# Output stores of a decay-attention and two-MLP kernel: one store of both batches, or one store per batch

## The chip, the core and the metric

The kernel runs on one core of a Trainium2 chip. The time is the device time of one execution in microseconds; the figure of the kernel before is the median of three runs. The profile is one profiled execution on the same kind of core, and all positions in it are microseconds from the start of its span.

## The reference

Three parts follow one another. Attention with an exponential decay runs over blocks of 64 positions, with a state carried from block to block, for 2 batches, 8 heads, 768 positions and 64 values per head. Its output is laid out as 1536 rows (batch, then position) of 512 values. Two MLPs follow.

```python
for b in range(nb):                       # blocks of 64 positions
    intra = einsum('bhij,bhjd->bhid', einsum('bhic,bhjc->bhij', qb, kb) * Dmask, vb)
    inter = einsum('bhid,bhde->bhie', qb * lam_pow, kv_state)
    out[:, :, sl] = intra + inter
    kv_state = lam_block * kv_state + einsum('bhsd,bhse->bhde', kb * rev_pow, vb)
x = out.transpose(0, 2, 1, 3).reshape(1536, 512)
h = x @ w_in;   x = (h * clip(h + 3, 0, 6) / 6) @ w_out       # first MLP, 512 -> 2048 -> 512
h = x @ w_in2;  out = maximum(0.01 * h, h) @ w_out2           # second MLP
```

## The kernel before

**Tiling.** The 1536 tokens are cut into three token tiles of 512 (`NTT` = 3), and each token tile holds 256 positions of both batches. Inside a token tile the tokens stand in four pieces (`SPT` = 4) of 128: 64 positions of batch 0 and the same 64 positions of batch 1. The hidden width of 2048 is cut into 16 slices of 128, which are grouped into blocks (`BLOCKS`). For each layer the work goes over blocks, in a block over token tiles, and in a token tile over the block's slices. One step is one slice on one token tile: a first product (`gemm1`, line 427, 12 matmuls), the gate on ScalarE and VectorE (lines 435 to 462), and a second product (`gemm2`, line 485, 12 matmuls) into four PSUM banks. Each fp32 operand is kept in two parts, so a product takes three matmuls.

**Sums.** When a block is done for a token tile, `collect` (line 496) adds each PSUM bank to the running sum `SUM[t][:, e, :]` in SBUF, one VectorE instruction of 128x512 for each of the four pieces e. In the second layer the 128 partitions of such a piece are tokens: partitions 0 to 63 are batch 0 (`own[0]`) and 64 to 127 are batch 1 (`own[1]`), and the 512 columns are the output values. In the last block of the second layer the sum is final, and `store(t, e)` (lines 510 to 513) sends it to the output. A store takes 128 rows of 2 KB from SBUF to two places of 64 contiguous rows each in the output, 768 rows apart. There are 12 stores, four for each token tile.

**Order.** The class `Order` is a list scheduler that runs while the program is built: it simulates engine times and due times and so fixes the order in which each engine gets its instructions. Every DMA of this kernel, load or store, is issued from SyncE's queue (SP). A store is added with `after=[c]`, c being the `collect` of its piece; nothing comes after a store, and no buffer is given back by it. The program ends (line 584, the end of the tile context) when SP has seen all DMAs land and the engines have met.

## Time and profile before

| | |
|---|---|
| median of 3 runs | 625.24 us (624.1 to 626.78) |
| profiled execution, span from first to last instruction | 622.5 us |
| profiled execution, time outside the span | the page gives none |
| TensorE matmul busy | 581.2 us (93%) |
| VectorE busy | 414.1 us (67%) |
| ScalarE busy | 272.4 us (44%) |
| GpSimd busy | 50.3 us (8%) |
| read from HBM, written to HBM | 45.88 MB, 3.15 MB |

The page's rows of tenths cut the span into 40 slices of 15.6 us; a digit is the busy share of an engine, and the DMA row is the mean busy share of the core's 16 DMA engines. The three runs and the profiled execution are different executions; the difference of 2.7 us between the median and the span holds what lies before the first and after the last instruction, and the spread from run to run.

### The profile page before, as it was taken

What the parts mean: (1) busy time and instruction counts of PE and PEld (TensorE: products, weight loads), DVE (VectorE), ACT (ScalarE), POOL (GpSimd) and SP (SyncE); (2) the same over time, 40 slices, a digit from 0 to 9 for tenths busy, and PEclk for the clock granted to TensorE, in tenths of its full rate; (3) what the DMA queues carried; (4) which work ended last, traced back from release to release, by engine and by line L of the source; (5) the groups of instructions that cost most, each with busy time, mean ns of one, the idle gap of its engine ahead of it and who ended that gap; (6) DMA issues with size and microseconds to landing.
All of it is one profiled execution on the core that took longest, in us unless ns stands there. A gap on an engine that the chain in (4) does not pass through costs nothing.

```text
span 622.5 us, 8825 instructions
## 1 busy us (share of the span) xinstructions
PE 581.2 (93%) x3562; PEld 483.2 (78%) x3562; DVE 414.1 (67%) x654; ACT 272.4 (44%) x460; POOL 50.3 (8%) x43
## 2 busy tenths in 40 slices
PE   7778799999999999999999999999999999999950
PEld 6568777888888888888888888888888888888840
DVE  8999999879479926985289962886469423442420
ACT  2356556775256424653266643672255222222200
POOL 3853540000000000000000000000000000000000
PEclk8978999999999999999999999999999999999985
DMA  8745652333103300330013120221011000001111
GB/s 285 241 156 184 203 173 75 112 120 105 65 35 115 122 0 23 113 120 16 2 35 135 68 101 1 95 108 68 2 58 44 1 1 1 0 12 51 49 47 46
DMA packets 16193, 49.60 MB, mean 80 GB/s; under 512 B 1944, under 2 KB 1944, under 8 KB 16152
## 3 DMA queue, kind: packets, MB, share of 16 engines
q1 hardware_dynamic: 16152, 49.03, 22.8%
q8 instruction: 28, 0.46, 0.3%
q14 instruction: 13, 0.11, 0.1%
HBM read 45.88 MB, written 3.15 MB: 79 GB/s over the span
## 4 chain that ended last, share of the span: by engine, by line
PE 86%; DVE 7%; DMA 3%; issue 0%; SPq 0%; DVEq 0%
PE h L427 42%; PE acc L485 35%; PE a L485 6%; DMA raw<-w 2%; DVE t L381 1%; DVE t L383 1%; PE a L273 1%; PE a L292 1%; DVE r L264 1%; PE a L258 1%; DVE t L373 1%; DVE xl L304 1%; DVE t L370 1%; DMA vs<-vv 1%; DVE sum L496 0%
## 5 line engine op out<-in xcount | busy, mean ns | idle before, releaser
L427 PE MATMUL h<-xh,wh 128*128 128x512 f32 (+1 forms) x396 | 153.3, 387 | 1.2 <-DVE xl L304 1.2
L427 PE MATMUL h<-xl,wh 128*128 128x512 f32 (+1 forms) x396 | 152.7, 386 | 0.2 <-DVE xl L304 0.2
L427 PE MATMUL h<-xh,wl 128*128 128x512 f32 (+1 forms) x396 | 152.6, 385 | 0.0
L427 PEld LDWEIGHTS h<-xh,wh 128*128 128x128 f32 x396 | 75.5, 191 | 16.1 <-ACT t L364 1.4
L452 ACT ACTIVATE gh<-u 128x512 fp32r<-128x512 f32 (+1 forms) x99 | 61.2, 620 | 61.0 <-DVE u L446 32.6
L427 PEld LDWEIGHTS h<-xh,wl 128*128 128x128 f32 x396 | 75.5, 191 | 14.7
L427 PEld LDWEIGHTS h<-xl,wh 128*128 128x128 f32 x396 | 75.4, 191 | 14.7 <-DVE xl L304 0.3
L446 DVE TENSOR_TENSOR u<-u,h 128x512 f32<-128x512 f32 x48 | 32.8, 684 | 65.1 <-ACT u L437 65.1
L437 ACT ACTIVATE u<-h 128x512 f32<-128x512 f32 x48 | 28.7, 598 | 105.7 <-PE h L427 105.5
L485 PE MATMUL acc<-gh,wh 128*128 128x512 f32 (+1 forms) x178 | 68.1, 383 | 2.8 <-DVE xl L304 2.8
L485 PE MATMUL acc<-gl,wh 128*128 128x512 f32 (+1 forms) x178 | 67.1, 377 | 0.0
L485 PE MATMUL acc<-gh,wl 128*128 128x512 f32 (+1 forms) x178 | 66.9, 376 | 0.0
L435 ACT ACTIVATE u<-h,three 128x512 f32<-128x512 f32 (+1 forms) x51 | 33.8, 663 | 73.1 <-PE h L427 72.9
L485 PE MATMUL acc<-wh,gh 128*128 128x512 f32 x160 | 62.2, 389 | 0.0
L485 PE MATMUL acc<-wl,gh 128*128 128x512 f32 x160 | 62.2, 389 | 0.0
L485 PE MATMUL acc<-wh,gl 128*128 128x512 f32 x160 | 62.2, 389 | 0.0
L391 ACT CAST wh<-t 128x512 fp32r<-128x512 f32 x64 | 39.5, 621 | 51.8 <-DVE t L383 45.5
L444 DVE SCALAR_TENSOR_TENSOR u<-u,h 128x512 f32<-128x512 f32 (+1 forms) x51 | 33.2, 652 | 26.9 <-ACT u L435 26.7
L383 DVE CUSTOM_DVE_ANT_0 t<-t,c 128x1024 uint16<-128x1024 uint16 x64 | 48.6, 760 | 2.2
L496 DVE TENSOR_TENSOR sum<-acc,sum 128x512 f32<-128x512 f32 x60 | 39.3, 684 | 16.1 <-PE acc L485 16.1
L381 DVE SCALAR_TENSOR_TENSOR t<-raw,t 128x512 uint32<-128x512 uint32 x64 | 47.6, 744 | 1.4
L360 ACT ACTIVATE c<-raw 128x512 uint32<-128x512 uint32 x64 | 42.7, 667 | 8.6 <-DMA raw<-w 8.6
(75 smaller groups left out, 759.1 us busy)
## 6 DMA issues: line engine op xcount, KB each, us to landing
raw<-w SPq DMA_DIRECT2D x64, 512.0 KB
q<-qkk SPq DMA_DIRECT2D x12, 512.0 KB
vs<-vv SPq DMA_DIRECT2D x24, 128.0 KB
out<-sum SPq DMA_DIRECT2D x12, 256.0 KB
k<-qkk SPq DMA_DIRECT2D x11, 256.0 KB
lam_sb<-lam SPq DMA_DIRECT2D x1, 4.0 KB
```

What stands on the lines that cost most here:

```text
L360: nc.scalar.activation(out=CV[h][1], in_=RAW[h][:, :, 0], func=AF.Copy, scale=2.0 ** -29)
L381: nc.vector.scalar_tensor_tensor(out=t, in0=RAW[h][:, :, 1], scalar=0xC0000000, in1=t, op0=ALU.bitwise_and, op1=ALU.bitwise_or)
L383: nc.vector.tensor_tensor(out=t, in0=t, in1=c, op=ALU.add)
L391: nc.scalar.copy(out=cut(*h, 0), in_=CV[h][0].bitcast(F32))
L427: nc.tensor.matmul(ps, a[:, 0, ws], x[:, k, :], start=(n == 0), stop=(n == 3 * KC - 1))
L435: nc.scalar.activation(out=U[s], in_=PH[s], func=AF.Relu, bias=three, scale=1.0)
L437: nc.scalar.activation(out=U[s], in_=PH[s], func=AF.Copy, scale=0.01)
L444: nc.vector.scalar_tensor_tensor(out=g, in0=U[s], scalar=6.0, in1=PH[s], op0=ALU.min, op1=ALU.mult)
L446: nc.vector.tensor_tensor(out=g, in0=U[s], in1=PH[s], op=ALU.max)
L452: nc.scalar.activation(out=G[s][0], in_=U[s], func=AF.Copy, scale=1.0 / 6.0 if steps[s][0] == 0 else 1.0)
L485: nc.tensor.matmul(ACC[e], a, x, start=(first and n == 0), stop=(last and n == 2))
L496: nc.vector.tensor_tensor(out=acc, in0=ps, in1=acc, op=ALU.add)
```

## The change

A store of 128 rows becomes two stores of 64 rows, one for each batch, each from one half of the partitions to 64 contiguous rows of the output. For the token tiles 0 and 1 both are issued from SP. For the last token tile the one of batch 0 is issued from SP and that of batch 1 from ScalarE's queue (ACT). The comments of the file are taken out too, with the line numbers kept up to line 510.

```diff
     def store(t, e):
         c0 = (t * SPT + e) * C
-        rows = out.rearrange("(b s) m -> b s m", b=B)[:, c0:c0 + C, :]
-        return lambda _: nc.sync.dma_start(out=rows, in_=SUM[t][:, e, :])
+
+        def fn(_):
+
+            for b in range(B):
+                queue = nc.scalar if b and t == NTT - 1 else nc.sync
+                queue.dma_start(out=out[b * S + c0:b * S + c0 + C, :], in_=SUM[t][own[b], e, :])
+        return fn
```

On SP's queue the end of the program reads as follows; `raw` are the weights, `sum_100` to `sum_102` the sums of the token tiles 0 to 2, and the shape is that of the transfer. Lines with - are of before, with + of the changed kernel.

```order
 L232 DMA vs<-vv 64x512 x2
 L353 DMA raw<-w 128x1024 x52
-L513 DMA out<-sum_100 2x64x512 x4
-L513 DMA out<-sum_101 2x64x512 x4
-L513 DMA out<-sum_102 2x64x512 x4
-L584 UNCONDITIONAL_BRANCH
+L517 DMA out<-sum_100 64x512 x8
+L517 DMA out<-sum_101 64x512 x8
+L517 DMA out<-sum_102 64x512 x4
+L589 UNCONDITIONAL_BRANCH
```

Twelve transfers with three dimensions become twenty with two, behind the same last weight load. On ScalarE, at the end of its program, where `u` and `gh` belong to the gate of the last steps:

```order
 L437 ACTIVATE u<-h 128x512
 L452 ACTIVATE gh<-u 128x512
-L584 UNCONDITIONAL_BRANCH
+L517 DMA out<-sum_102 64x512 x4
+L589 UNCONDITIONAL_BRANCH
```

Four transfers stand behind ScalarE's last arithmetic instruction, and nothing but the end of the program behind them. On TensorE, VectorE and GpSimd the order of the instructions is the same in both kernels.

## Rows read from the trace of the kernel before

**Rows 1.** The page: the span, TensorE's line, and of the 40 slices TensorE's busy tenths, the DMA engines' tenths and what they moved.
```profile
span 622.5 us, 8825 instructions
...
PE   7778799999999999999999999999999999999950
...
DMA  8745652333103300330013120221011000001111
GB/s 285 241 156 184 203 173 75 112 120 105 65 35 115 122 0 23 113 120 16 2 35 135 68 101 1 95 108 68 2 58 44 1 1 1 0 12 51 49 47 46
DMA packets 16193, 49.60 MB, mean 80 GB/s; under 512 B 1944, under 2 KB 1944, under 8 KB 16152
```

**Rows 2.** The chain of work that ended last, its last pieces in order of time: start, length, what.
```profile
588.55 2.04 PE acc L485 x9
590.59 2.72 PE h L427 x12
593.31 4.09 PE acc L485 x18
597.40 0.02 issue
597.43 2.73 DVE sum L496 x4
```

**Rows 3.** The waits of SP's queue over the whole span: total, times, longest.
```profile
SPq L513 <- DVE sum L496: 117.8, 8, 86.4
SPq L584 <- DMA out<-sum: 13.4, 1, 13.4
```

**Rows 4.** The timeline of SP's queue around the stores (several answers; start, length from the first to the end of the last, count): the first store behind VectorE's sum that it waits for, the last token tile's four, and the last one of these; at the end ScalarE's last instruction.
```profile
553.91 0.69 DVE L496 TENSOR_TENSOR sum<-acc,sum 128x512 f32<-128x512 f32 x1 [1.31 <-PE acc L485]
...
554.63 0.65 SPq L513 DMA_DIRECT2D out<-sum  x1
...
598.15 9.87 SPq L513 DMA_DIRECT2D out<-sum  x4
...
603.29 4.73 SPq L513 DMA_DIRECT2D out<-sum  x1
...
594.76 0.63 ACT L452 ACTIVATE gh<-u 128x512 fp32r<-128x512 f32 x1 [0.75 <-DVE u L446]
```

**Rows 5.** Stretches of the span: length, busy time of the five engines (instructions), granted clock, DMA share of the 16 engines, GB/s. Four of the stretches have stores alone on the queue; the last one has loads alone.
```profile
558.00:576.00 18.00, 18.00 (x81) 14.90 (x80) 6.87 (x11) 4.32 (x7) 0.00 (x0) 1.00 0.13 50
577.00:598.00 21.00, 21.00 (x94) 17.38 (x94) 7.79 (x12) 4.92 (x8) 0.00 (x0) 1.00 0.13 49
598.00:604.00 6.00, 1.43 (x7) 0.85 (x5) 2.16 (x4) 0.00 (x0) 0.00 (x0) 0.85 0.13 40
604.00:620.00 16.00, 0.00 (x0) 0.00 (x0) 0.00 (x0) 0.00 (x0) 0.00 (x0) 0.50 0.13 51
4.00:16.00 12.00, 9.56 (x157) 7.71 (x156) 11.74 (x16) 2.99 (x6) 4.71 (x3) 0.86 1.04 357
```

**Rows 6.** The DMA view of the stretch from 604 to 620 us: packets by size. Packets under 512 B are the completions.
```profile
DMA packets 406, 0.82 MB, mean 51 GB/s; under 512 B 6, under 2 KB 6, under 8 KB 406
```

**Rows 7.** The DMA view of two stretches in 40 slices: GB/s from 554.6 to 556.6 us (0.05 us each), where the first store begins, and from 618 to 622 us (0.1 us each), where the last one ends.
```profile
GB/s 0 0 0 0 0 0 0 0 0 0 0 0 0 0 0 0 0 0 0 0 0 0 0 0 0 82 0 82 0 0 82 0 0 0 82 0 0 0 0 82
...
GB/s 41 61 61 41 41 61 61 41 41 61 61 41 41 61 61 41 41 61 61 41 41 61 61 41 41 61 61 41 41 61 21 0 0 0 0 0 0 0 0 0
```

**Rows 8.** A load of 64 rows of 2 KB (`vs`, line 232) on an otherwise empty queue: SP's timeline, and the DMA view from 89.5 to 90.5 us (40 slices of 0.025 us) with its packets.
```profile
88.39 1.62 SPq L232 DMA_DIRECT2D vs<-vv  x2
...
GB/s 0 0 0 0 0 0 164 164 0 0 164 82 410 164 82 246 164 410 246 246 410 492 328 246 492 164 246 164 82 0 82 0 0 0 0 0 0 0 0 0
DMA packets 80, 0.13 MB, mean 131 GB/s; under 512 B 16, under 2 KB 16, under 8 KB 80
```

**Rows 9.** Lines 513 (stores), 232 (loads of 64 rows) and 353 (loads of weights) on SP's queue: time that an issue took in ns (shortest, median, longest), start of the first and the last. Then a pair of loads of 64 rows as it most often stands in the timeline.
```profile
L513 SPq DMA_DIRECT2D out<-sum x12: 502/522/4749, 554.6 to 603.3; - x12
L232 SPq DMA_DIRECT2D vs<-vv x24: 465/588/1189, 3.1 to 88.9; - x24
L353 SPq DMA_DIRECT2D raw<-w x64: 327/328/536, 2.6 to 467.9; - x64
...
62.67 1.11 SPq L232 DMA_DIRECT2D vs<-vv  x2
```

**Rows 10.** SP's semaphore instructions at the end of the program (line 584), times in ns, start of the first and the last in us.
```profile
L584 SPq EVENT_SEMAPHORE  x7: 17/28/28, 621.4 to 622.5; - x7
```

**Rows 11.** Two pieces of the chain of work: matmuls beside a weight load that runs from 108.6 to 110.2 us, and without one.
```profile
109.80 8.19 PE h L427 x36
...
128.87 2.72 PE h L427 x12
```

## The prediction

> **What bounds the kernel now.** I began with the page's slices. TensorE's digits are 9 from the seventh slice on, then 5 and 0 in the last two, while the DMA row, empty before, goes on with 1s to the very end at 46 to 51 GB/s [rows 1]. So the kernel has two bounds one after the other: TensorE for about 600 us, and then something that moves few bytes slowly. The chain of work closes with four VectorE sums that end at 597.43 + 2.73 = 600.16 us [rows 2], yet the span is 622.5. The chain holds no store: the last 22.3 us are outside it, and the reader must find them in the waits of SP's queue. There the end of the program (L584) waits once, for 13.4 us, for a DMA of the output [rows 3]; before that, SP is busy issuing: the last tile's four stores take 9.87 us to issue, the last from 603.29 to 608.02 [rows 4]. After 604 us no compute engine does anything; only stores run [rows 5].

> How fast do they run? The DMA share is 0.13 of 16 engines, that is 2.1 engines, at 51 GB/s, about 25 GB/s for a busy engine [rows 5]. Loads in the first 16 us keep all sixteen busy at 357 GB/s, 22 GB/s each [rows 5]. So a store's engine is not slow; there are only two. The packets say the same: 16 us move 0.82 MB, about three stores, with 6 completions, two for a store [rows 6], while a load of 64 rows has 16 [rows 8]. A store of 256 KB takes 262 / 51 = 5.1 us; twelve take 62 us, but the first starts at 554.63 [rows 4] and the sums end at 600.16. The stores are a backlog from 558 us on (0.13 in every stretch, [rows 5]), and the end of the kernel is the end of that backlog, at 618 + 3.05 = 621.05 us [rows 7].

> [...]

> **The change part by part.** *Splitting.* Twelve stores become 24 of 64 rows, 128 KB. The trace of before has no such store, but its mirror image: a `vs` load of 64 rows of 2 KB. It was issued at 88.39, its packets run from 89.65 to 90.28 (slices 6 to 30 of 0.025 us), 0.63 us for 131 KB, or 208 GB/s with ramps [rows 8]. I take the store to be as fast: a busy engine did 25 GB/s in stores and 22 in loads. At this rate a tile's 1.05 MB take 5.0 us at most, where the next tile's first sum is some 21 us away, so no backlog reaches the last tile.

> *The last tile, step by step.* The last sum still ends at 600.16, as nothing on TensorE, VectorE or ScalarE's arithmetic moves. From a sum to the store's issue is 554.63 - 554.60 = 0.03 us [rows 4]. From issue to the first packet: 555.85 - 554.63 = 1.22 us for a store [rows 4, 7], 89.65 - 88.39 = 1.26 for the load [rows 8]; I take 1.22. Data of the last pair, 262 KB: at sixteen engines of 25 GB/s, 400 GB/s, 0.65 us; one half behind the other at the load's pace, 1.26 us. I take 1.0. From the last packet to SP's release: 621.4 - 621.05 = 0.35 us [rows 7, 10]. From there to the end of the span 622.5 - 621.4 = 1.1 us [rows 10]. Sum: 600.16 + 0.03 + 1.22 + 1.0 + 0.35 + 1.1 = 603.9 us, against the span's 622.5: 18.6 us less, with 18.4 to 19.0 from the data's two ends.

> *Issue.* Each new DMA costs its queue an issue: 0.52 us is the median for stores, 0.59 for 64-row loads, and a pair of those takes 1.11 to 1.62 us, so 0.55 to 0.81 each [rows 8, 9]. The last tile's sums come every 2.73 / 4 = 0.68 us [rows 2], so one queue with one issue per sum keeps up or falls behind by at most 3 x 0.13 = 0.4 us. The 4.7 us of the slowest issue before [rows 9] I read as a queue that was full of the backlog; with the backlog goes that. The eight extra issues of tiles 0 and 1 stand on SP behind the last weight load at 467.9 [rows 9]; nothing is queued behind them but later stores. On ScalarE the four issues wait for VectorE's sums, and behind them stands only the end of the program; its last gate instruction ends at 595.39 [rows 4], so no arithmetic waits. I cost both at nothing.

> *The second queue.* ACT's issue of a DMA isn't in the trace. Below: nothing, each queue issuing on its own. Above: the two share what makes an issue long, so that eight run one after the other from 598.15: at 0.55 each they end at 602.55, at 0.81 at 604.65, instead of at 600.7 (600.19 + 0.52): 1.9 to 4.0 us later. I take nothing: 64 weight loads took 0.327 at the shortest and 0.328 at the median [rows 9], whether the DMA engines were full or idle, which looks like time of the issuing queue's own and not of something shared. I keep 4.0 for the range.

> *Stores of tiles 0 and 1 in short bursts.* They run beside matmuls, at up to sixteen engines instead of two. The matmuls beside a weight load took 8.19 / 36 = 0.2275 us, without one 2.72 / 12 = 0.2267 [rows 11], so a burst costs TensorE nothing that I can count; even at 0.0008 us more for each of the 94 matmuls of such a stretch it is 0.1 us.

> The runs: the sum is made in the span, 622.5; the median is 625.24, 2.7 us more, which I leave as it is. 625.24 - 18.6 = 606.6 us.

> **The rivals.** *Issues in a row.* The two queues issue one after the other: 1.9 to 4.0 us are given back, 608.5 to 610.6. For it: pairs of 64-row loads on one queue took up to 1.62 us [rows 8]. Against it: that is one queue, and in most pairs 1.11.

> *Writing is slower than reading with many engines.* Nothing in the trace shows more than two engines writing. At 100 GB/s the last tile's 1.05 MB from 598.15 + 1.22 = 599.37 end at 609.9, the span at 611.3, and the time is 614.0; at 200 GB/s it is 608.8. Against it: two engines write at the load's rate per engine.

> *The rate is the writing's, and the split only adds DMAs.* If 51 GB/s is what this core writes, whatever the shape, the backlog ends where it does now, and twelve further DMAs are strung on it. Each costs between nothing (the store boundaries between 604 and 620 leave the rate at 51, [rows 5]) and one issue of 0.52: 625.2 to 631.5 us; I price it at 631.5. It is slower by more than 0.5% (3.1 us, about what a measurement of this kernel can tell from no change) once a DMA costs 0.26 us. For it: no row shows a faster store. Against it: the share of 0.13 and two completions per store [rows 5, 6], which name engines and not a memory that is slow.

> [...]

> **How the numbers follow.** Forecast 0.82, 604.8 to 608.0 by itself (the data's ends, and 1.3 us for the spread of the runs, 624.1 to 626.78). Issues in a row 0.08; slower writing 0.05; no gain 0.05, of that 0.03 slower and 0.02 within 0.5%. The first three are faster by over 0.5%, together 0.95. The range goes from 604.8 to 610.6: it holds the forecast, the issues in a row and the mild end of slower writing.

> **What would show it.** The span near 603.9; the last sum at 600.2 as before; SP's wait at the end for the output near 2 us instead of 13.4, and no issue of a store above 1.2 us. Completions: 24 stores with sixteen each instead of twelve with two, so packets under 512 B go from 1944 to 1944 - 24 + 384 = 2304. Between the tiles' stores the DMA row falls to 0. Four stores on ACT at about 598.15, 598.8, 599.5 and 600.2. I am wrong if stores still show 0.13 and 51 GB/s, if completions stay at two, if ACT's issues begin late behind SP's, or if the sums end later than 600.2.

## The result, and the profile after

The changed kernel takes 606.72 us (median of four runs, 605.23 to 606.95), beside 624.67 us for the kernel before in the same runs; the ratio is 0.970, with a 95% interval of 0.968 to 0.973. 606.6 was predicted. The profiled execution has a span of 604.7 us and took 606.48 us, so 1.8 us lie outside its span.

The page of the changed kernel, as in [rows 1]: span, TensorE's tenths, the DMA engines' tenths, GB/s, packets.

```profile
span 604.7 us, 8843 instructions
...
PE   7778889999999999999999999999999999999996
...
DMA  8745653334203410322002231034102100000232
GB/s 287 254 133 186 207 172 108 104 109 139 70 2 104 137 38 1 104 73 102 1 1 89 86 118 56 1 105 128 47 1 69 36 1 1 1 0 18 52 70 69
DMA packets 16553, 49.60 MB, mean 82 GB/s; under 512 B 2304, under 2 KB 2304, under 8 KB 16512
```

TensorE's 9s now reach to the slice before the last, and the last one has a 6: the tail with a 5, a 0 and 1s under it is gone. The small packets went from 1944 to 2304, which is 360 more: 24 stores with sixteen completions each where twelve had two.

The end of the chain of work, which answers to [rows 2], and SP's wait for the output, which answers to [rows 3]:

```profile
593.55 4.09 PE acc L485 x18
597.64 0.02 issue
597.67 2.73 DVE sum L496 x4
```
```profile
SPq L589 <- DMA out<-sum: 2.8, 3, 1.5
```

The last sum ends at 600.40 us, 0.24 later than before; in the fourteen profiled executions of this document it ends between 599.80 and 601.59, with no order by kernel. From there to the end of the span it is 604.7 - 600.4 = 4.3 us, where it was 22.3. The difference of these two tails, 18.0 us, is the whole gain. I use this tail below to compare runs, since it leaves out how late the last sum ends. SP waits three times for the output, 2.8 us in all, where it waited once for 13.4.

The last tile's stores in the timeline of the two queues, then line 517 (issue time in ns, first and last start in us), then two stretches (columns as in [rows 5]): the same one as before, and the one in which the last tile's bytes move.

```profile
598.39 2.51 SPq L517 DMA_DIRECT2D out<-sum  x4
...
598.39 2.75 ACTq L517 DMA_DIRECT2D out<-sum  x4
```
```profile
L517 SPq DMA_DIRECT2D out<-sum x20: 466/548/601, 554.9 to 600.4; - x20
...
L517 ACTq DMA_DIRECT2D out<-sum x4: 555/587/703, 598.4 to 600.6; - x4
```
```profile
577.00:598.00 21.00, 21.00 (x95) 17.38 (x94) 7.55 (x12) 4.93 (x8) 0.00 (x0) 1.00 0.23 51
...
599.50:603.30 3.80, 0.17 (x1) 0.00 (x0) 0.90 (x2) 0.00 (x0) 0.00 (x0) 0.85 0.88 276
```

Both queues begin with the first sum, at 598.39. SP keeps pace with the sums, its last issue beginning at 600.4; ScalarE's queue falls some 0.2 us behind, to 600.6. The last tile's 1.05 MB take 3.8 us at 276 GB/s, with 0.88 of the sixteen engines busy; before, they took some 20 us at 51 GB/s and 0.13 [rows 5].

The DMA view of the first tile's stores, 554 to 574 us in 40 slices of 0.5 us, and of the last tile's, 599 to 604 us in slices of 0.125 us:

```profile
GB/s 0 0 0 0 197 205 123 33 0 0 49 201 213 201 225 184 217 201 82 0 0 0 0 0 0 0 0 0 0 0 0 0 0 0 0 0 0 0 0 0
...
GB/s 0 0 0 0 197 262 229 82 246 213 443 328 443 361 344 131 328 229 328 360 311 229 312 295 328 229 262 279 377 361 393 279 131 82 0 0 0 0 0 0
```

The first tile's bytes are out at 563.5, and the queue is empty until the next tile; before, the backlog ran through. The last byte of all leaves at 603.25.

### The profile page after: what moved, and what is told of

Read it like the earlier page. It is cut to its first block, busy times and chain, and to the rows that moved or that the text cites. A ratio compares the mean times of both kernels' runs of the same rounds, so it can differ in the third digit from the quotient of the medians.

```text
span 604.7 us, 8843 instructions
## 1 busy us (share of the span) xinstructions
PE 581.4 (96%) x3562; PEld 483.2 (80%) x3562; DVE 413.5 (68%) x654; ACT 272.4 (45%) x460; POOL 50.3 (8%) x43
## 2 busy tenths in 40 slices
DMA packets 16553, 49.60 MB, mean 82 GB/s; under 512 B 2304, under 2 KB 2304, under 8 KB 16512
## 4 chain that ended last, share of the span: by engine, by line
PE 85%; DVE 11%; DMA 2%; issue 1%; ACT 1%; SPq 0%; DVEq 0%; ACTq 0%
PE h L427 41%; PE acc L485 35%; PE a L485 7%; DVE t L381 2%; DVE t L383 1%; DVE r L264 1%; DVE t L370 1%; DVE t L373 1%; DVE r L246 1%; PE a L273 1%; DVE xl L304 1%; PE a L292 1%; DMA raw<-w 1%; DMA vs<-vv 1%; DMA lam_sb<-lam 0%
## 5 line engine op out<-in xcount | busy, mean ns | idle before, releaser
L427 PEld LDWEIGHTS h<-xh,wl 128*128 128x128 f32 x396 | 75.5, 191 | 14.6
```

The lines of the kernel that those rows point to most:

```text
L427: nc.tensor.matmul(ps, a[:, 0, ws], x[:, k, :], start=(n == 0), stop=(n == 3 * KC - 1))
```

## The experiments

| run | a store | stores | completions per store | tail us | time us |
|---|---|---|---|---|---|
| before | 2x64x512 | 12 | 2 | 22.3 | 624.67 |
| the change | 64x512, two queues | 24 | 16 | 4.3 | 606.72 |
| e2 | 64x512, one queue | 24 | 16 | 5.5 | 608.21 |
| e3 | last tile split only | 16 | 2 and 16 | 4.3 | 606.79 |
| e4 | 48 and 16 rows | 48 | 16 and 16 | 5.2 | 608.26 |
| e5 | 62 and 2 rows | 48 | 2 and 2 | 22.1 | 624.61 |
| e6 | 61 and 3 rows | 48 | 1 and 3 | 77.4 | 680.74 |
| e7 | 2x64x512, two queues | 12 | 2 | 22.4 | 625.50 |
| e8 | 2x64x256 | 24 | 2 | 23.7 | 625.29 |
| e9 | first two tiles split only | 20 | 16 and 2 | 22.5 | 624.09 |
| e10 | 57 and 7 rows | 48 | 3 and 7 | 14.6 | 617.87 |
| e11 | 64x2x512, one queue | 12 | 16 | 3.5 | 605.99 |

**The change once more, as a mark.**

> The changed kernel once more, as the mark for the three runs beside it. Both theories: 606.7 us, ratio to the kernel before 0.970.

607.01 us, 0.971 (0.970 to 0.973), tail 4.2 us.

**The number of rows, with all else as in the change.** Three kernels cut each 64 rows at n = 48, 62 or 61. Everything that the rivals name is kept: contiguous places, two queues, more and smaller stores.

```diff
-                queue.dma_start(out=out[b * S + c0:b * S + c0 + C, :], in_=SUM[t][own[b], e, :])
+                for lo, hi in ((0, n), (n, C)):
+                    queue.dma_start(out=out[b * S + c0 + lo:b * S + c0 + hi, :], in_=SUM[t][b * C + lo:b * C + hi, e, :])
```

> Each store of 64 rows cut once more, into 48 and 16 rows, 48 stores in all; by the theory both still use sixteen engines. Eight issues on each queue for the last tile instead of four: 1.0 to 2.0 us more than the change, 607.7 to 608.7. Rival (each further store costs its own start, some 1.2 us on the engines): 24 more of them, 8 of these in the last tile, so 610 to 616. It is also the mark for the cut into 62 and 2 rows.

> Each store of 64 rows cut into 62 and 2 contiguous rows, on the same queues as in the change. Theory: 62 and 2 are both split over two engines, so every piece of 256 KB takes 5.1 us again and the old time is back, 623 to 628, with two completions per store. Rival (what helps is that a store goes to one contiguous place, or that there are more stores): as with 48 and 16 rows, 606 to 610.

> Each store of 64 rows cut into 61 and 3 contiguous rows. Theory: 61 rows go over one engine, and always the same one, 61 x 0.08 = 4.9 us, 24 of them 117 us from 556 on, with the 3 rows some 2 us more: the span ends near 676, the time is 675 to 682, and completions are one and three per store. If the engine changed from store to store it would be 606 to 630. Rival (contiguous place or more stores): 606 to 610.

48 and 16 rows: 608.26 us, 0.974 (0.972 to 0.976), 1.25 us above the change, as the theory had it, though the two intervals overlap; the tail is 1.0 us longer. 62 and 2 rows, a single run: the old time, 624.61 beside 624.85 for the kernel before. 61 and 3 rows: 680.74, also a single run, 56 us slower than before. Between the first two cuts only the place of the cut differs, and that costs 16 us. The same stretch after the last sum in the two slow ones, 62 rows first:

```profile
606.00:618.00 12.00, 0.00 (x0) 0.00 (x0) 0.00 (x0) 0.00 (x0) 0.00 (x0) 0.50 0.13 51
```
```profile
606.00:618.00 12.00, 0.00 (x0) 0.00 (x0) 0.00 (x0) 0.00 (x0) 0.00 (x0) 0.50 0.07 26
```

0.13 of sixteen engines and 51 GB/s is two engines, the same reading as before. 0.07 and 26 GB/s is one engine. The run stays at these two figures from 600 to 660 us and takes 680.74 us, where the expectation has 606 to 630 for an engine that changes, so I take it to be the same one for every piece of 61 rows.

**A count in between.**

> Each store of 64 rows cut into 57 and 7 rows. Theory: 57 rows go over three engines and 7 over seven, so the busiest engine has 2 x (19 + 1) = 40 packets in a piece of 256 KB, 3.2 us at 0.08 us; the last tile's four pieces take 13 us from 599.6, the span ends near 614 and the time is 614 to 618, with 3 and 7 completions. A rival by which only the lowest counts are slow: 607 to 610.

617.87 us in a single run, beside 625.72 for the kernel before: inside the range of the theory, near its upper end, with ten completions for a pair, as three and seven would give. From 603 to 612 us it has a share of 0.29 and 81 GB/s, where two engines had 0.13 and 51. So the low counts are not a class of their own here. That the busiest engine's packets set the time is my estimate, 614 to 618 us, which the run meets without showing the engines one by one.

**The second queue alone.** No split; pieces 1 and 3 of the last tile from ScalarE's queue.

```diff
-        return lambda _: nc.sync.dma_start(out=rows, in_=SUM[t][:, e, :])
+        def fn(_):
+            queue = nc.scalar if e % 2 and t == NTT - 1 else nc.sync
+            queue.dma_start(out=rows, in_=SUM[t][:, e, :])
+        return fn
```

> No split: a store of both batches as before, those of pieces 1 and 3 of the last tile on ScalarE's queue. Theory: both queues feed the same two engines, so the backlog ends where it did, 624 to 626. Rival (the second queue carries the gain): the last tile's four stores take half as long, 614 or less.

625.50 against 624.85 before: nothing gained. The last tile's issues no longer block, two of them in 1.87 us on SP's queue and two in 1.89 on ScalarE's where four took 9.87 [rows 4], but all the time comes back as one wait at the end:

```profile
SPq L588 <- DMA out<-sum: 21.5, 1, 21.5
```

**More stores without more engines.** The cut goes through the columns instead of between the batches; `rows`, here and in the next two runs, is the output side of the kernel before.

```diff
+            for i in range(2):
+                queue = nc.scalar if i and t == NTT - 1 else nc.sync
+                queue.dma_start(out=rows[:, :, i * DM // 2:(i + 1) * DM // 2], in_=SUM[t][:, e, i * DM // 2:(i + 1) * DM // 2])
```

> Each store of both batches cut into two halves of its columns (2x64 rows of 1 KB) instead of by batch, the second half of the last tile on ScalarE's queue: 24 stores of 128 KB as in the change. Theory: the output side still has 2 in front, so two engines; 625 where a packet of 1 KB takes half the time of one of 2 KB, up to 652 where it takes 0.06 us. Rival (more and smaller stores in flight help): 606 to 615.

625.29: 24 stores of 128 KB on two queues, as in the change, and no gain. Packets of 1 KB moved at nearly the rate of those of 2 KB, 48 GB/s at a share of 0.14 where the others had 51 at 0.13 [rows 5]:

```profile
606.00:618.00 12.00, 0.00 (x0) 0.00 (x0) 0.00 (x0) 0.00 (x0) 0.00 (x0) 0.50 0.14 48
```

**Which of the stores count.** Two runs split only the last tile, or only the first two, and store the others as before.

```diff
+            if not (t == NTT - 1):          # the other run: t < NTT - 1
+                nc.sync.dma_start(out=rows, in_=SUM[t][:, e, :])
+                return
```

> Token tiles 0 and 1 stored as before, in one store of both batches; only the last tile split, on two queues. Theory: the two tiles' stores still creep at two engines, 5.1 us each, but tile 1's end near 598.5, just before the last tile's begin, so the whole gain stays: 606.7, at most 1 us more. Rival (the backlog of all three tiles has to be gone): 610 or above.

> The counterpart of the run that split only the last tile: tiles 0 and 1 split, the last tile's four stores as before. Theory: the backlog of the first tiles is gone, so the last tile's stores start at once, but still take 4 x 5.14 = 20.6 us at two engines: from 599.6 to 620.2, span 621.7, time 623.7 to 624.7; only 0 to 1 us of the gain. Rival (the backlog is what costs): 606 to 612.

Last tile only: 606.79, 0.970 (0.968 to 0.972), all of the gain. First two only: 624.09 beside 625.72, a single run each, with the same tail as before, 22.5 us. There the last tile's stores had no store in front of them, and still one of their issues took 4.73 us, as long as the longest of the kernel before [rows 9]:

```profile
L516 SPq DMA_DIRECT2D out<-sum x4: 517/2194/4731, 597.8 to 603.1; - x4
```

In the run that split only the last tile, tile 1's stores still creep at two engines up to the last tile's, as the stretch shows:

```profile
577.00:598.00 21.00, 21.00 (x95) 17.38 (x94) 7.32 (x12) 4.92 (x8) 0.00 (x0) 1.00 0.13 49
```

So the stores of the first two tiles cost nothing in themselves. The stores of two tiles fit, barely, beside the other tile's matmuls; what is paid for is the part that has no work left to hide it.

**One queue instead of two.**

```diff
-                queue = nc.scalar if b and t == NTT - 1 else nc.sync
-                queue.dma_start(out=out[b * S + c0:b * S + c0 + C, :], in_=SUM[t][own[b], e, :])
+                nc.sync.dma_start(out=out[b * S + c0:b * S + c0 + C, :], in_=SUM[t][own[b], e, :])
```

> All 24 stores on SyncE's queue, none on ScalarE's. Theory (the number of DMA engines that a store uses sets the time): eight issues of 0.55 us follow one another from 598.4, the last ends at 602.8 instead of 601.2, so 0.9 to 1.9 us are given back, 607.6 to 608.6. Rival (the second queue carries the gain): the last tile's eight stores queue up behind one another and 5 us or more are given back, 612 or above.

608.21 us, 0.973 (0.971 to 0.975), 1.2 us above the change; the intervals overlap, and the tail of the profiled execution, 5.5 us against 4.2 to 4.35 in the three of the change, goes the same way. The second queue is the small part of the change. The last tile's issues now run to 603.41, 0.62 us each. The timeline, and a stretch in which one half-store after the other moves:

```profile
598.44 4.97 SPq L515 DMA_DIRECT2D out<-sum  x8
```
```profile
600.00:602.00 2.00, 0.00 (x0) 0.00 (x0) 0.45 (x1) 0.00 (x0) 0.00 (x0) 1.00 0.94 208
```

Sixteen engines are busy 94% of the time, and yet they move 208 GB/s, no more. But 131 KB in 0.62 us, the pace of the issues, is 211 GB/s as well. The trace gives the time from issue to landing too, here of the first two of the eight and of the last four:

```profile
DMA to landing us min/median/max: 2.3/2.3/2.4
```
```profile
DMA to landing us min/median/max: 2.3/2.4/2.4
```

It doesn't grow, so the stores don't pile up behind one another: the moving keeps up with the issues, and 208 GB/s is the pace at which they came. Whether issues closer together would have moved more, this run doesn't show.

**Sixteen engines without a split.** The eleventh run goes back to the kernel before, twelve stores of both batches on SP's queue, and changes only in which order the tokens of a piece stand, position before batch. The matmuls don't see the order of the tokens; two lines change.

```diff
-            xh, xl = (x.rearrange("p k (c b i) -> p k c b i", c=SPT, b=2)[:, :, c % SPT] for x in X[c // SPT])
+            xh, xl = (x.rearrange("p k (c i b) -> p k c b i", c=SPT, b=2)[:, :, c % SPT] for x in X[c // SPT])
...
-        rows = out.rearrange("(b s) m -> b s m", b=B)[:, c0:c0 + C, :]
+        rows = out.rearrange("(b s) m -> s b m", b=B)[c0:c0 + C]
```

> No split and no second queue: twelve stores of both batches on SyncE's queue as before, but with the tokens of a piece ordered position first and batch second, so that the output side is 64x2x512 instead of 2x64x512. Same bytes, same number of stores, same two places. Theory: 64 in front gives sixteen engines, sixteen completions per store, the gain of the change or a little more (four issues of 0.52 us instead of eight): from the end of the last sum to the end 4.0 to 4.6 us, 606 to 608, unless the attention's writes at a stride of two cost more. Rival (a store to two places is slow, or the number of stores counts): 624 or above.

> The changed kernel beside the run with interleaved batches: 606.7 to 607.0 us, 4.2 us from the end of the last sum to the end.

605.99 us, 0.971 (0.968 to 0.973), beside 606.96 for the change, 0.972 (0.970 to 0.974): the gain of the change with half the stores and one queue. The two can't be told apart by their times; in the tails this one is shorter, 3.5 against 4.3 us. The store still goes to two places, so a contiguous place is not what helped. Its stores in the timeline, and a stretch of the last tile:

```profile
598.50 2.58 SPq L513 DMA_DIRECT2D out<-sum  x4
```
```profile
600.00:602.00 2.00, 0.00 (x0) 0.00 (x0) 0.51 (x1) 0.00 (x0) 0.00 (x0) 1.00 1.03 381
```

381 GB/s from one queue, and that is no more than the pace at which the sums come, 262 KB every 0.68 us; from issue to landing no store takes longer than the others, so none waits for another:

```profile
DMA to landing us min/median/max: 2.4/2.4/2.5
```

The change with two queues has this (run e1; the profiled execution of the result has 0.94 and 306 GB/s in the same stretch):

```profile
600.00:602.00 2.00, 0.36 (x2) 0.00 (x0) 1.09 (x2) 0.00 (x0) 0.00 (x0) 1.00 0.86 253
```

## Why the prediction was right

**The bound.** Two engines for a store, and a tail made of their stores: shown three ways, by one engine (e6, a tail of 77.4 us), by two with everything else of the change (e5, 22.1), and by sixteen with nothing else of it (e11, 3.5). My picture of one backlog of twelve stores was too wide: the stores of the first two tiles end about when the last tile's begin, and the tail is made by the last tile's four alone. Splitting these alone gave the whole gain (e3), splitting the others gave no shorter tail (e9).

**Splitting.** Sixteen completions and no backlog, as said. The trace of before shows no store on sixteen engines, only the load of 64 rows; the runs show it, with a DMA share of 0.86 to 0.94 for half-stores (e1, e2). The 400 GB/s at one end of my data term no run shows as their rate: the last tile's moved at 276 in the change. The mirror image, the load of 64 rows at 208 GB/s, was a fair model: half-stores one behind the other moved at 208 too (e2), though there the issues come no faster. The model also held a warning that I passed over, below.

**The last tile's sum.** From the first sum, which ends about 598.36, to the issue it is 0.03 us; from there to the first packet at 599.5, 1.1 us against 1.22. From the last byte to the end of the span it is 604.7 - 603.25 = 1.45 us, as the two last terms say (0.35 + 1.1). The data term was the one that was mis-sized. The last sum ends at 600.40, so by my terms the last pair's packets begin at 600.40 + 0.03 + 1.22 = 601.65, and the last byte left at 603.25: 1.6 us, where I took 1.0, and outside the two ends that I gave, 0.65 and 1.26. These 0.6 us are the difference between the 18.6 us that I forecast and the 18.0 by which the tail got shorter.

The 1.6 us are not the last pair's own. From 601.65 on this was still moved:

```profile
601.65:603.30 1.65, 0.00 (x0) 0.00 (x0) 0.00 (x0) 0.00 (x0) 0.00 (x0) 0.67 0.81 267
```

That is 0.44 MB, and a pair is 0.26: some 0.18 MB of earlier pairs stood in front. The time from issue to landing grows in the same way; here the two stores of the first pair, then the last three issued:

```profile
DMA to landing us min/median/max: 2.3/2.5/2.7
```
```profile
DMA to landing us min/median/max: 3.2/3.2/3.2
```

At 276 GB/s a pair takes 0.95 us, near the 1.0 that I took, but the sums bring a new pair every 0.68 us. So each pair begins some 0.27 us further behind, about 0.8 us for the fourth; this is an estimate, and with the pair's own 0.95 it gives 1.75 us where 1.6 were measured. What my sum left out is this queue: I priced the last pair as if the three before it were gone.

That the time came out at 606.72 against 606.6 is luck in part. The span was 0.8 us longer than the 603.9 of the sum, and the 2.7 us that I added outside it were 0.9 too many. In every run on record with both figures, 1.7 to 1.9 us lie outside the span; the rest of the 2.7 came from setting the median of three runs beside the span of another execution. One of my signs of being wrong, sums that end after 600.2, was met by 0.2 us, inside the spread given above; it was too tight to tell anything. The bounds of the forecast alone add up to 604.9 and 608.2 rather than 604.8 and 608.0, and nothing hangs on that.

**Issue.** An issue on ScalarE's queue takes 0.59 us at the median, 0.70 at most; none on either queue is above 1.2. The 4.7 us of before I had put down to the backlog of all tiles; they belong to the last tile's own slow stores, as they stay where only the first two tiles are split (e9). The two queues issue side by side, four in 2.51 and four in 2.75 us from the same start, so the rival of issues in a row is out. For one queue with one issue per sum I allowed 0.4 us of delay; such a queue keeps pace (e11, the last issue at 600.5 behind a sum that ends at 600.51). With two per sum (e2) the tail is 1.2 us longer.

**Stores beside matmuls.** TensorE's busy time is 581.4 us, 581.2 before: nothing lost.

**The other rivals.** Writing was not slower than reading here: the last tile's half-stores moved at 276 GB/s where loads moved at 357 [rows 5], but whole stores moved at 381 (e11). That 51 GB/s is the writing's own rate is refuted by every run with sixteen completions. Beside one store of both batches that already has sixteen engines, two halves gain nothing: 605.99 us (e11) against 606.96 for the change.

## What to carry to other kernels

Read the end of a kernel past the last piece of the chain of work: a long wait of the DMA queue (13.4 us here, [rows 3]) with a low, steady DMA share (0.13, [rows 5]) is worth reading as a transfer that runs on few engines, and here its completions, the small packets of the page, said on how many. In these runs stores with 16, 48 or 64 rows in front ran on sixteen engines, and those with 2, 61 or 62 on one or two, by their completions and rates, with the cut into 57 and 7 between them (81 GB/s): a 2 in front left 51 GB/s where a 64 in front gave 208 to 381. Reordering the rows, where the computation allows it, cured that here without more transfers (e11, 605.99 us). Only the stores behind the last computation cost time here: split alone they gave 606.79 us (e3), and with only the others split it was 624.09 (e9).

## What was not expected

Stores from 64 of the 128 partitions did not reach the rate of stores from all, though the sixteen engines were nearly always busy in both: a share of 0.94 with 208 GB/s (e2), of 0.88 with 276 (the change), and of 1.03 with 381 (e11). With sums at the same pace, whole stores kept up at 381 GB/s (e11), while both halves at once from two queues fell behind, at 276 over the last tile's bytes (the change). One half after the other made 208 (e2), but there the issues came no faster; the load of 64 rows, alone on the queue, had 208 as well [rows 8]. So the pairs piled up in the last tile, from 2.3 to 2.7 us from issue to landing for the first of them to 3.2 for the last. What holds an engine back there, no run of these shows.

The tokens' order of the eleventh run costs ScalarE a little: eight of its thirteen copies of the attention's output (line 307) take 622 ns at the median where they took 586, and the whole kernel doesn't show it.
